# Two MoE products as seven block products each, in place of eight, on one Trainium2 core

## The chip, the core and the metric

The kernel runs on one core of one Trainium2 chip. The metric is device time in microseconds, as the median of some runs. The core has a matrix engine (PE, its weight loads shown apart as PEld), three engines for elementwise work (DVE, ACT, POOL), and SP, which here issues all data transfers. Every engine executes its own instructions in order; waits between engines go through semaphores.

## What is computed

Attention with a sigmoid in place of softmax for 8 batches, 12 heads, 448 positions and head size 64; its result, laid out as 3584 tokens by 768, goes through two matrix products with a gate between them. All is float32.

```
scores = scale * np.matmul(q, k.transpose(0, 1, 3, 2)) - np.log(S)
attn = 1.0 / (1.0 + np.exp(-scores))
attn_out = np.matmul(attn, v)
x = attn_out.transpose(0, 2, 1, 3).reshape(B * S, H * D)
h = x @ w_in                              # 768 -> 2048
g = h * np.clip(h + 3.0, 0.0, 6.0) / 6.0
out = g @ w_out                           # 2048 -> 768
```

The weights arrive as 64-bit floats and are turned into float32 on the chip.

## The kernel before

**Attention** runs in steps: 21 to a batch, 168 in all. A step is four score products (L162) into a PSUM tile `sc` with two buffers, one sigmoid on ACT (L164), and, two steps behind, four products of the result with v (L194). Float32 products run in passes, so the trace has two records for each, 16 records to a step. After each pair of heads, ACT copies one half of the result (L210), DVE adds the other (L211), and DVE splits the sum into a high and a low part of type fp32r (L214, L215).

**The first MoE product** (`moe_in`, L256) works on blocks of 512 tokens (T) and 128 output rows: six chunks of d_model times three products (high by high, high by low, low by high), 18 matmuls of 128x128 weights with 512 moving columns, into one PSUM bank. There are 7 token blocks by 16 row blocks: 2016 matmuls. ACT and DVE make the gate (L260, L261) and SP stores it to DRAM (L263). It is interleaved with attention by batches: three batches, two token blocks, then one batch and one block in turn, and the last block at the end.

**The second product** (`moe_out`, L391) reads the gate back (L347, 1 MB at a time), splits it (L351 on ACT, L352 on DVE), and makes 48 matmuls of 512 columns for each of 42 output tiles: again 2016. DVE scales the result (L398) and SP stores it.

**The weights** are decoded by a chain of one ACT and six DVE or POOL operations, and split (`join_f64`, `split_f32` for w_in, L51 to L67; `split_over` for w_out, L74 to L86). w_in is decoded during the first three batches and the first two blocks; w_out at the end of the first product and the start of the second.

PE, ACT, DVE and POOL follow the order in which the program is written until the last attention batch is done; after that only PE does, and a scheduler sets the others. SP's order is the scheduler's throughout.

## Time and profile before

| | |
|---|---|
| median of 3 runs | 1183.84 us (1183.82 to 1184.26) |
| span of the profiled execution | 1182.4 us, 1.4 us under the median: its own time is not listed apart |
| PE busy | 1172.5 us, 99% |
| DVE, ACT, POOL busy | 427.7, 378.4 and 64.5 us |
| granted PE clock | 1.000 of full |
| moved through DRAM | 129 MB, mean 109 GB/s |

The page gives for each group of instructions its busy time and the mean duration of one in ns. Matmuls are pipelined: the duration of one is longer than the distance to the next, and the distance is what counts. A row of the chain of waits is start, duration and what ran; "xN" counts records.

### The profile page before, as it was taken

The page shows a single profiled execution, that of the slowest core. Times are in us where ns is not written, and L with a number is a line of the kernel's source. Part 1 is how long each engine was busy: PE and PEld are TensorE (multiplying, and loading weights), DVE is VectorE, ACT ScalarE, POOL GpSimd, SP SyncE. Part 2 cuts the span into 40 slices and gives each one's busy share as a digit, 9 for nine tenths or more (in the row PEclk, how much of TensorE's full clock was granted, in tenths as well). Part 3 has the DMA queues.
Part 4 walks back from the last instruction along what each step waited for, and adds up shares of the span by engine and source line. Part 5 has one row for each costly group of instructions (what it writes and reads, how often), then busy time and mean ns, then how long its engine had stood idle before and what let it go on. Part 6 is the DMA issues. An engine that isn't in the chain of part 4 may idle for free.

```text
span 1182.4 us, 16264 instructions
## 1 busy us (share of the span) xinstructions
PE 1172.5 (99%) x6720; PEld 856.1 (72%) x6720; DVE 427.7 (36%) x762; ACT 378.4 (32%) x506; POOL 64.5 (5%) x70
## 2 busy tenths in 40 slices
PE   8999999999999999999999999999999999999998
PEld 3336888748847855874884788888888888888887
DVE  3777772242122123114112699860302203030300
ACT  6885331271163144126116454230201002020200
POOL 1333441000000000000000000000000000000000
PEclk9999999999999999999999999999999999999999
DMA  7655441141132123114112578540321304040000
GB/s 243 197 185 158 161 152 72 63 134 61 71 105 91 63 91 113 63 66 138 63 63 66 176 244 294 167 171 27 109 82 39 154 27 160 27 169 25 21 27 27
DMA packets 52010, 128.99 MB, mean 109 GB/s; under 512 B 9184, under 2 KB 15328, under 8 KB 48352
## 3 DMA queue, kind: packets, MB, share of 16 engines
q1 hardware_dynamic: 51936, 127.95, 31.8%
q8 instruction: 53, 0.87, 0.3%
q14 instruction: 21, 0.17, 0.0%
HBM read 87.56 MB, written 40.37 MB: 108 GB/s over the span
## 4 chain that ended last, share of the span: by engine, by line
PE 99%; ACT 0%; DMA 0%; DVE 0%; issue 0%
PE ph L256 39%; PE po L391 39%; PE sc L162 11%; PE pv L194 11%; ACT a L164 0%; DMA qk<-qk 0%; DVE o L398 0%
## 5 line engine op out<-in xcount | busy, mean ns | idle before, releaser
L256 PE MATMUL ph<-x,wi 128*128 128x512 f32 x2016 | 458.8, 389 | 0.0
L256 PEld LDWEIGHTS ph<-x,wi 128*128 128x128 f32 x2016 | 377.9, 188 | 82.5 <-issue 4.2
L391 PE MATMUL po<-gh,woh 128*128 128x512 f32 x672 | 261.4, 389 | 0.0
L391 PE MATMUL po<-gl,woh 128*128 128x512 f32 x672 | 261.4, 389 | 0.0
L391 PE MATMUL po<-gh,wol 128*128 128x512 f32 x672 | 261.4, 389 | 0.0
L164 ACT ACTIVATE a<-sc,bias_s 128x896 f32<-128x896 f32 x168 | 168.6, 1008 | 53.2 <-PE sc L162 52.0
L261 DVE SCALAR_TENSOR_TENSOR g<-g,ph 128x512 f32<-128x512 f32 x112 | 76.9, 687 | 273.3 <-ACT g L260 273.3
L260 ACT ACTIVATE g<-ph,bias 128x512 f32<-128x512 f32 x112 | 77.2, 689 | 285.1 <-PE ph L256 277.5
L162 PE MATMUL sc<-qk 64*64 64x448 f32 x1344 | 157.5, 545 | 6.2 <-DMA qk<-qk 4.3
L194 PE MATMUL pv<-a,v 64*64 64x448 f32 x1344 | 154.0, 537 | 0.0
L351 ACT CAST gh<-gr 128x2048 fp32r<-128x2048 f32 x28 | 53.6, 1915 | 293.1 <-PE po L391 292.3
L391 PEld LDWEIGHTS po<-gl,woh 128*128 128x128 f32 x672 | 126.1, 188 | 26.2
L391 PEld LDWEIGHTS po<-gh,wol 128*128 128x128 f32 x672 | 126.1, 188 | 26.2
L391 PEld LDWEIGHTS po<-gh,woh 128*128 128x128 f32 x672 | 126.1, 188 | 26.1
L398 DVE TENSOR_SCALAR o<-po 128x512 f32<-128x512 f32 x42 | 29.0, 690 | 294.1 <-PE po L391 294.1
L162 PEld LDWEIGHTS sc<-qk 64*64 64x64 f32 x1344 | 49.5, 134 | 84.3 <-issue 60.3
L194 PEld LDWEIGHTS pv<-a,v 64*64 64x64 f32 x1344 | 50.3, 133 | 76.7 <-issue 71.7
L352 DVE TENSOR_TENSOR gl<-gr,gh 128x2048 fp32r<-128x2048 f32 x28 | 64.1, 2289 | 27.6 <-ACT gh L351 27.6
L211 DVE TENSOR_TENSOR x<-pv,y 128x448 f32<-128x448 f32 (+6 forms) x78 | 32.5, 416 | 113.2 <-ACT y L210 93.0
L61 POOL TENSOR_TENSOR wis<-wis 128x384 f32<-128x384 f32 x32 | 32.4, 1012 | 98.2 <-DVE wis L58 95.8
L215 DVE TENSOR_TENSOR x<-x,x 128x448 fp32r<-128x448 f32 (+6 forms) x78 | 32.8, 420 | 2.7
L67 POOL TENSOR_TENSOR wi<-wis,wi 128x384 fp32r<-128x384 f32 x32 | 32.2, 1019 | 20.2 <-ACT wi L66 17.2
(29 smaller groups left out, 309.0 us busy)
## 6 DMA issues: line engine op xcount, KB each, us to landing
gd<-g SPq DMA_DIRECT2D x112, 256.0 KB, 2.4
gr<-gd SPq DMA_DIRECT2D x28, 1024.0 KB, 5.4
qk<-qk SPq DMA_DIRECT2D x48, 448.0 KB, 3.8
wis<-wi SPq DMA_DIRECT2D x32, 384.0 KB, 3.4
ws<-wo SPq DMA_DIRECT2D x24, 512.0 KB, 4.4
outT<-o SPq DMA_DIRECT2D x42, 256.0 KB, 2.0
v<-vP SPq DMA_DIRECT2D x24, 224.0 KB, 2.6
v<-vP SPq DMA_DIRECT2D x24, 192.0 KB, 3.0
```

The lines of the kernel that those rows point to most:

```text
L61: nc.gpsimd.tensor_tensor(out=a, in0=a, in1=b, op=ALU.add)
L162: nc.tensor.matmul(out, k[halves[r], at_k], q[halves[r]], start=True, stop=True)
L164: nc.scalar.activation(a, sc[:, :, :S], AF.Sigmoid, bias=bias_s, scale=scale)
L194: nc.tensor.matmul(pv[p][r][halves[j], :S], v, a[halves[r], int(r != j) if c is None else j], start=first, stop=last)
L211: nc.vector.tensor_tensor(out=x, in0=p1[:, q0 : q0 + w], in1=y, op=ALU.add)
L215: nc.vector.tensor_tensor(out=xl, in0=x, in1=xh.bitcast(F32), op=ALU.subtract)
L256: nc.tensor.matmul(ph, w[:, cc], x, start=(n == 0), stop=(n == 3 * NCC - 1))
L260: i1 = nc.scalar.activation(g, ph, AF.Relu, bias=bias_3, scale=1.0)
L261: i2 = nc.vector.scalar_tensor_tensor(out=g, in0=g, scalar=6.0, in1=ph, op0=ALU.min, op1=ALU.mult)
L351: nc.scalar.copy(gh, gr)
L352: nc.vector.tensor_tensor(out=gl, in0=gr, in1=gh.bitcast(F32), op=ALU.subtract)
L391: nc.tensor.matmul(po[t, ec], w[:, fc], x[:, u], start=(fc == 0 and n == 0), stop=(fc == NFC - 1 and n == 2))
```

## The change

Both products are made by Winograd's form of Strassen's scheme. A weight matrix is cut into four quarters A11, A12, A21, A22, and the moving matrix into four quarters B11, B12, B21, B22, where the columns are two batches (a *pair*, `p`, 0 to 3; 448 columns each) and the rows the two halves of the contracted dimension. Sums of quarters come first: S1 = A21 + A22, S2 = S1 - A11, S3 = A11 - A21, S4 = A12 - S2, and T1 = B12 - B11, T3 = B22 - B12, T2 = T3 + B11, T4 = B21 - T2. Then there are seven products in place of eight:

M1 = A11 B11, M2 = A12 B21, M3 = S4 B22, M4 = A22 T4, M5 = S1 T1, M6 = S2 T2, M7 = S3 T3.

The results are C11 = M1 + M2, C21 = M1 + M6 + M7 + M4, C22 = M1 + M6 + M7 + M5, C12 = M1 + M6 + M5 + M3. All sums are float32, and each product still consists of three fp32r products.

**Attention** comes first, all 168 steps. x of the first pair stays on the chip; its sums are made by DVE (`x_sums`) and its seven operands split (`x_split`: a cast on ACT, a subtraction on DVE), at steps 45 to 62. x of the other three pairs goes to DRAM and comes back later. In the same time w_in is decoded (16 units of 768 values a partition, one in six steps), its sums are made by POOL, and quarters and sums are stored to DRAM; so are A11 and A12 of w_out.

**The first product** then runs in 112 *slots* (`product`), one for each of 7 products by 16 *quads* (4 row groups by 4 pairs); a slot is 18 matmuls of 448 columns. Accumulators are PSUM tiles A (two buffers), B and D (one each). A holds M1, then M6, M7 and M4 added on top, and ACT copies it in between (`copied`); B holds M2; D holds M5, then M3 on top. DVE adds the copies (`added`), ACT and DVE make the gate (`relu`, `gate`), POOL makes T2 and T3 of the gate (`g_sums`), and SP stores six pieces for each quad. The weights of each slot are loaded five slots ahead and split three slots ahead (`w1_load`, `w1_split`). At the seams between pairs, the seven operands of the next pair are split one by one (in `x_split`), each after the last use of the old one.

**The second product** runs in 56 *units*: seven products (order M1, M2, M6, M7, M5, M4, M3), four pairs, two halves of the contraction; a unit is 36 matmuls of 448 columns. Its moving operand is loaded three units ahead and split two units ahead (`g_load`, `g_split`); for M5 and M4 it is also a difference of two stored pieces. A21 and A22 of w_out are decoded in units 0 to 11, POOL makes the sums in units 6 and 12 (`w2_sums`), SP stores them one unit later, and the weights of each product are loaded back and split at its seam (units 8, 16, ..., 48).

All five engines, SP too, now follow the order written. In the rows below the names are the program's, and the number behind the last underscore is a running count.

**ACT during attention.** Before, some 30 steps in, while w_in is decoded: the sigmoids (L164), copies of the attention result (L210) and the w_in chain (L51, L66).

```order
L164 ACTIVATE a_738<-sc_733,bias_s 128x896
L164 ACTIVATE a_749<-sc_744,bias_s 128x896
L66 CAST wi_595<-wis_596 128x384
L51 ACTIVATE wis_670<-wis_670 128x384
L164 ACTIVATE a_776<-sc_771,bias_s 128x896
L210 COPY y_0_783<-pv_9_714 128x64
L210 COPY y_1_789<-pv_9_714 128x384
L164 ACTIVATE a_800<-sc_795,bias_s 128x896
```

At most two short operations stand between two sigmoids. Now, from step 50 on: sigmoids (L177), copies (L202), decoding (L50) and the casts of the first pair's operands (L69).

```order
L177 ACTIVATE a_948<-sc_943,bias_s 128x896
L69 CAST x_0_952<-xr_0_260 128x1344
L202 COPY y_959<-pv_903 128x448
L177 ACTIVATE a_967<-sc_962,bias_s 128x896
L177 ACTIVATE a_983<-sc_978,bias_s 128x896
L69 CAST x_2_987<-xr_1_735 128x1344
L177 ACTIVATE a_1001<-sc_996,bias_s 128x896
L177 ACTIVATE a_1012<-sc_1007,bias_s 128x896
L69 CAST x_1_1014<-xr_1_416 128x1344
L202 COPY y_1022<-pv_973 128x448
```

A cast of 1344 values stands between every second sigmoid and the next, seven times.

**DVE at a seam between pairs in the first product.** Before, at the end of a batch: the last attention result is added and split, then only gates (L261) follow while the product runs.

```order
L211 TENSOR_TENSOR x_0_4746<-pv_41_4709,y_0_4747 128x384
L214 CAST x_5_4037<-x_0_4746 128x384
L215 TENSOR_TENSOR x_5_4037<-x_0_4746,x_5_4037 128x384
L211 TENSOR_TENSOR x_1_4752<-pv_41_4709,y_1_4753 128x64
L214 CAST x_5_4756<-x_1_4752 128x64
L215 TENSOR_TENSOR x_5_4756<-x_1_4752,x_5_4756 128x64
L261 SCALAR_TENSOR_TENSOR g_0_4778<-g_0_4778,ph_0_4759 128x512
```

No operand is split while the product runs. Now, from the slot of M1 of the last quad of a pair on: operands of the next pair (x_0 is B11, x_1 B21, x_2 B22), gates (L344), weights (w), sums (L362).

```order
L70 TENSOR_TENSOR x_0_4158<-xr_0_0_3572,x_0_4158 128x1344
L344 SCALAR_TENSOR_TENSOR g_6_4130<-g_6_4130,cD_4128 128x896
L70 TENSOR_TENSOR w_4164<-ws_4101,w_4164 128x768
L344 SCALAR_TENSOR_TENSOR g_6_4185<-g_6_4185,A_3937 128x896
L70 TENSOR_TENSOR w_4190<-ws_4132,w_4190 128x768
L362 TENSOR_TENSOR cB_4212<-B_4193,s_7_4156 128x896
L70 TENSOR_TENSOR x_1_4216<-xr_0_1_3574,x_1_4216 128x1344
L344 SCALAR_TENSOR_TENSOR g_7_4214<-g_7_4214,cB_4212 128x896
L70 TENSOR_TENSOR w_4223<-ws_4162,w_4223 128x768
L362 TENSOR_TENSOR cD_4244<-D_4081,u_6_4069 128x896
```

The last row reads the accumulator D that the next M5 overwrites, and all the others stand before it.

**ACT and SP in units 6 and 7 of the second product.** Before, ACT in the second product decodes the rest of w_out and then only casts gates:

```order
L74 ACTIVATE wa_3_6147<-ws_3_6146 128x512
L85 CAST woh_6108<-wa_0_6111 128x512
L85 CAST woh_6108<-wa_1_6123 128x512
L85 CAST woh_6108<-wa_2_6135 128x512
L85 CAST woh_6108<-wa_3_6147 128x512
L351 CAST gh_0_6432<-gr_0_6431 128x2048
```

The decoded parts lie in buffers of their own, and SP loads and stores no weights by way of DRAM. Now, ACT (with what each row waits for):

```order
L69 CAST gx_8_6391<-gr_8_6342 128x1792 [waits DMAHW2_49,DVE_49]
L50 ACTIVATE w2_2_1_6401<-wo_2_1_0_6351 128x512 [waits DMAHW3_49,DMAHW0_49,Pool_49]
L69 CAST gx_9_6450<-gr_9_6394 128x1792 [waits DMAHW4_49,DVE_49,PE_49]
L50 ACTIVATE w2_2_1_6401<-wo_2_1_1_6409 128x512 [waits DMAHW5_49]
L69 CAST w2_1_0_0_6471<-w2s_1_0_6411 128x512 [waits DMAHW6_49]
```

and SP:

```order
L452 DMA w2s_1_0_6411<-dw2_1_0_75 128x1536 [waits DMAHW7_49,DMAHW6_49,DVE_49]
L428 DMA gr_10_6453<-gd_1_1_0_101 128x1792 [waits Activation_49]
L536 DMA dw2_5_0_81<-w2r_0_0_6298 128x1536 [waits DMAHW0_49,Pool_49]
L536 DMA dw2_6_0_83<-w2_2_0_6069 128x1536 [waits DMAHW1_49]
L536 DMA dw2_4_0_79<-w2S1_0_6396 128x1536 [waits DMAHW2_49]
L536 DMA dw2_3_0_77<-w2_3_0_6236 128x1536 [waits DMAHW3_49]
L536 DMA dw2_7_0_85<-w2r_1_0_6300 128x1536 [waits DMAHW4_49,Pool_49]
L248 DMA wo_2_1_2_6467<-wo 128x1024 [waits DMAHW5_49,DVE_49]
```

`w2_2_1` takes the buffer of `w2r_0_0`, in which POOL makes S2 and which SP stores as `dw2_5_0`; behind the ACT row that waits for both stand the cast of unit 9's operand and those of M2's weights (`w2_1_0_0`).

The core of the diff; attention's own lines change little, and the old product functions go.

```diff
-    def moe_in(*blocks):
-        for i, (fc, t) in enumerate(itertools.product(range(NFC), blocks)):
...
-    def moe_out(t, ec, g):
...
+def sums(engine, a11, a12, a21, a22, s1, s2, s3, s4):
+
+    engine.tensor_tensor(out=s1, in0=a21, in1=a22, op=ALU.add)
+    engine.tensor_tensor(out=s3, in0=a11, in1=a21, op=ALU.subtract)
+    engine.tensor_tensor(out=s2, in0=s1, in1=a11, op=ALU.subtract)
+    engine.tensor_tensor(out=s4, in0=a12, in1=s2, op=ALU.subtract)
...
+    for q in range(n - 1):
+        seq += [(M1, q + 1), (M4, q), (M2, q + 1), (M3, q), (M6, q + 1), (M5, q + 1), (M7, q + 1)]
...
+    def ring(name, shape, dtype):
+        return dw.tile(shape, dtype, tag="ring", name=name, bufs=5)
...
+    def x_split(p, k):
+        x = xt[k].tile([P, 2, KC, S], F32R, tag="x", name=f"x_{p}_{k}")
+        split(nc, x[:, 0], x[:, 1], xr[p].pop(k))
+        xts[p, k] = x
...
+    for i, k in enumerate((B11, B22, B21, T3, T1, T2, T4)):
+        on(end0 + 6 + 2 * i, x_split, 0, k)
...
+    def product(i, q, n):
+
+        w, x = wr.pop(n), xts[q // NQ, MOVING[i]]
+        if i == M1:
+            acc["A", q] = bank("sc", 2, f"A_{q}")
+        if i == M2:
+            acc["B", q] = bank("pv0", 1, f"B_{q}")
+        if i == M5:
+            acc["D", q] = bank("pv1", 1, f"D_{q}")
+        t = acc["B" if i == M2 else "D" if i in (M5, M3) else "A", q]
+        for j in range(2):
+            m = 0
+            for kc in range(KC):
+                for wk, xk in ((0, 0), (0, 1), (1, 0)):
+                    nc.tensor.matmul(
+                        t[:, j, :S],
...
+    def copied(q, key):
+        acc[key, q] = temp("a", 4, f"{key}_{q}")
+        nc.scalar.copy(acc[key, q], acc["A", q][:, :, :S])
+
+    def added(q, key, name):
+        c = temp("y", 2, f"c{name}_{q}")
+        nc.vector.tensor_tensor(out=c, in0=acc[name, q][:, :, :S], in1=acc[key, q], op=ALU.add)
+        return c
...
+        for i in range(7):
+            at_slot(last[i, p - 1] + 1, x_split, p, MOVING[i])
...
+        for k, o in enumerate(others):
+            part = t[:, 2 * k : 2 * k + 2]
+            nc.vector.tensor_tensor(out=part, in0=part, in1=o, op=ALU.subtract)
...
+        at_unit(6 * h + 4, w2_reload, h)
+        at_unit(6 * h + 6, w2_sums, h)
+        at_unit(6 * h + 7, w2_store, h)
+    for k, i in enumerate(PHASES[1:]):
+        n = 8 * (k + 1)
+        at_unit(n - 2, w2_load, i, 0)
+        at_unit(n - 1, w2_load, i, 1)
+        at_unit(n - 1, w2_split, i, 0)
+        at_unit(n, w2_split, i, 1)
```

More of the change, by code (lines that the diff above doesn't have):

```diff
@@ new lines, in w2_unit @@
+    def w2_unit(k, h, ec, held):
+        st = staging(f"wo_{k}_{h}_{ec}", [P, FC * P, 2], I32)
+        nc.sync.dma_start(out=st, in_=wo[k, h, :, ec * FC * P : (ec + 1) * FC * P])
+        yield
+        if ec == 0:
+            held[k, h] = ring(f"w2_{k}_{h}", [P, EC, FC * P], F32)
+        yield from decode(nc, st, held[k, h][:, ec])
+        if ec == EC - 1 and k in (A11, A12):
+            nc.sync.dma_start(out=dw2[k, h], in_=held.pop((k, h)))
+    held = {}
+    todo = []
+    for u in range(4 * NQ):
+        todo.append((1 + 6 * u, 4, w1_unit(*divmod(u, 2), held)))
@@ new lines, in g_load @@
+    def g_load(n):
+        if n >= len(units):
+            return
+        i, p, h = units[n]
+        first, second = {T1: (B12, B11), T4: (B21, T2)}.get(MOVING[i], (MOVING[i], None))
+        t = gset[n % 3].tile([P, FC, S], F32, tag="gr", name=f"gr_{n}")
+        nc.sync.dma_start(out=t, in_=gd[p, first, h])
+        others = []
+        if second is not None:
+            for k in range(2):
+                o = ring(f"gr_{n}_{k}", [P, 2, S], F32)
+                nc.sync.dma_start(out=o, in_=gd[p, second, h][:, 2 * k : 2 * k + 2])
+                others.append(o)
+        gr[n] = t, others
@@ new lines, in w2_split @@
+    def w2_split(i, h):
+        st = w2s.pop((i, h))
+        for ec in range(EC):
+            w = xs.tile(
+                [P, 2, FC, P], F32R, tag="xT" if h else "xraw", name=f"w2_{i}_{h}_{ec}", bufs=3 if h else 5
+            )
+            flat = w.rearrange("p t c e -> p t (c e)")
+            split(nc, flat[:, 0], flat[:, 1], st[:, ec])
+            w2[i, h, ec] = w
+    last = {}
+    for n, (i, q) in enumerate(seq):
+        last[i, q // NQ] = n
+    first = {}
+    for n, (i, q) in reversed(list(enumerate(seq))):
+        first[q // NQ] = n
@@ new lines, in tile_kernel, with xt_close @@
+    for p in range(1, NPR):
+        at_slot(first[p - 1] + 2, x_load, p)
+        at_slot(first[p - 1] + 8, x_sum_start, p, first[p - 1] + 9)
+        for i in range(7):
+            at_slot(last[i, p - 1] + 1, x_split, p, MOVING[i])
+    end = len(seq)
+    for h in range(2):
+        at_slot(end - 12 + h, w2_load, M1, h)
+        at_slot(end - 10 + 2 * h, w2_split, M1, h)
+    def xt_close(*ks):
+        for k in ks:
+            xt_ctx[k].close()
+        g_open()
+    for n in range(LA):
+        pass
@@ new lines, in tile_kernel @@
+    for n in range(LA, LA + 2):
+        w1_load(n)
+    p_last = NPR - 1
+    for n, (i, q) in enumerate(seq):
+        for f, a in later.pop(n, []):
+            f(*a)
+        w1_load(n + LA + 2)
+        w1_split(n + LA)
+        product(i, q, n)
+        post(i, q, n)
+        if n == last[M6, p_last]:
+            xt_close(B11, T2)
+            g_load(0)
+        if n == last[M2, p_last]:
+            xt_close(T3, B21)
+            g_load(1)
+        if n == last[M6, p_last] + 2:
+            g_split(0)
+        if n == last[M2, p_last] + 2:
+            g_split(1)
@@ new lines, in tile_kernel @@
+    for n, (i, p, h) in enumerate(units):
+        if n < 2:
+            drain_later()
+        if n == 1:
+            while later:
+                drain_later()
+            tmp_ctx.close()
+            acc_ctx.append(ctx.enter_context(tc.tile_pool(name="acc", bufs=1, side="right", reuse_waits="tile")))
+        g_split(n + 2)
+        g_load(n + 3)
+        for f, a in plan.pop(n, []):
+            f(*a)
+        if h == 0:
+            po[p] = po_pool.tile([P, EC, 512], F32, tag="po", name=f"po_{i}_{p}")
+        x = gs.pop(n)
+        for ec in range(EC):
+            w = w2[i, h, ec]
+            for c in range(FC):
+                for wk, xk in ((0, 0), (0, 1), (1, 0)):
+                    nc.tensor.matmul(
+                        po[p][:, ec, :S],
+                        w[:, wk, c],
+                        x[:, xk, c],
+                        start=h == 0 and c == 0 and xk == 0 and wk == 0,
+                        stop=h == 1 and c == FC - 1 and wk == 1,
+                    )
+        if h == 1:
+            post2(i, p)
```

600 lines of the change are left out of this document (325 added, 275 removed).

## The prediction, as it was put on record

> **What bounds the kernel now.** I read the page's busy times and chain first, then the chain in order of time.
>
> ```profile
> PE 1172.5 (99%) x6720; PEld 856.1 (72%) x6720; DVE 427.7 (36%) x762; ACT 378.4 (32%) x506; POOL 64.5 (5%) x70
> PE 99%; ACT 0%; DMA 0%; DVE 0%; issue 0%
> PE ph L256 39%; PE po L391 39%; PE sc L162 11%; PE pv L194 11%; ACT a L164 0%; DMA qk<-qk 0%; DVE o L398 0%
> ```
> ```profile
> 0.73 3.52 DMA qk<-qk
> 4.30 4.76 PE sc L162 x24
> ...
> 99.41 2.25 PE pv L194 x24
> 101.66 130.82 PE ph L256 x576
> 232.49 0.96 PE sc L162 x8
> ...
> 264.82 65.50 PE ph L256 x288
> ...
> 721.69 456.97 PE po L391 x2016
> ```
>
> PE's matmuls set the end all along. The products take 456.97 / 2016 = 226.7 ns a matmul (130.82 / 576 = 227.1 in the first), 4032 of them 914 us. Attention takes 2.25 / 24 x 16 records = 1.50 us a step.
>
> Why 226.7 ns? Attention's rows tell the rate: four of its 64*64 records run side by side, so 24 in 2.25 us are 375 ns for four; if each streams its 448 columns twice, that is 2.4 columns a ns, and 512 columns would take 213.3. So 13.3 ns come on top. The weight loads could be the cause:
>
> ```profile
> L256 PEld LDWEIGHTS ph<-x,wi 128*128 128x128 f32 x2016 | 377.9, 188 | 82.5 <-issue 4.2
> 740.56 0.39 PE L391 MATMUL po<-gh,woh 128*128 128x512 f32 x1
> 740.57 0.19 PEld L391 LDWEIGHTS po<-gl,woh 128*128 128x128 f32 x1
> 740.79 0.39 PE L391 MATMUL po<-gl,woh 128*128 128x512 f32 x1
> ```
> ```profile
> 101.59 0.30 PEld L256 LDWEIGHTS ph<-x,wi 128*128 128x128 f32 x2 [0.70 <-issue]
> ```
>
> A load starts as its predecessor's matmul starts and lasts 188 ns; the next matmul comes 39 ns after its end. But in the last row two loads of 188 ns end within 0.30 us, so one follows the other by 0.11. A load is then not what 226.7 ns wait for; the columns are.
>
> **Part one: the matmuls.** The order keeps their number (112 x 18 + 56 x 36 = 4032), so it does what it says, and takes the columns from 512 to 448. No row has 448 columns with full-size weights. Lower end: all of 226.7 scales, 198.3 ns. Upper end: nothing does, 226.7. I take the 13.3 ns as fixed, 186.7 + 13.3 = 200.0: a slot is 3.6 us, a unit 7.2, each product 2016 x 0.2 = 403.2 us, together 806.4 against 914.
>
> **Part two: attention.** 168 steps x 1.503 = 252.5 us; the first load 4.3; the cold start costs 4.76 - 2.25 = 2.5. A batch that starts alone, as from 232.49 to 264.82, takes 32.3 us for 21 steps of 1.503 (31.6); five such starts fall away, some 4 us against before. What is new is the load on ACT and DMA.
>
> ```profile
> L164 ACT ACTIVATE a<-sc,bias_s 128x896 f32<-128x896 f32 x168 | 168.6, 1008 | 53.2 <-PE sc L162 52.0
> L74 ACT ACTIVATE wa<-ws 128x512 f32<-128x512 f32 x24 | 16.2, 677 | 43.9 <-DMA ws<-wo 38.9 <-DVE wol L86 3.0 <-DVE wa L77 1.9
> L51 ACT ACTIVATE wis<-wis 128x384 f32<-128x384 f32 x32 | 17.7, 556 | 2.1 <-DVE wis L57 2.1
> L351 ACT CAST gh<-gr 128x2048 fp32r<-128x2048 f32 x28 | 53.6, 1915 | 293.1 <-PE po L391 292.3 <-DMA gr<-gd 0.7
> L85 ACT CAST woh<-wa 128x512 fp32r<-128x512 f32 x24 | 14.8, 616 | 13.4 <-DVE wa L84 13.3
> L210 ACT COPY y<-pv 128x448 f32<-128x448 f32 x12 | 6.3, 526 | 1.2 <-PE pv L194 1.2
> ```
>
> From L351 and L85 a cast costs 0.183 us + 0.846 ns a value: 1.32 us for an operand (1344), 0.83 for a slot's weights (768), 1.70 for a unit's (1792). From L74 and L51, decoding 768 values costs ACT 0.92. In the 14 steps from 50 on (21.0 us) ACT has 14 sigmoids (14.1), seven casts (9.2), 2.3 decodings (2.1) and four copies (2.1): 27.5. Two score buffers give 1.2 us of slack (a step lasts 1.5, a sigmoid 1.0, and the second next step waits for it). So PE waits 6.5 - 1.2 = 5.3 us. Bounds: 0 if idle time around absorbs it, 8 if DVE, as full there (the pair's four sums and seven subtractions, 17 us by the slope below, beside 19 of decoding and adding in 30), adds its own.
>
> ```profile
> 60.00:70.00 10.00, 10.00 (x112) 3.79 (x108) 8.07 (x19) 8.91 (x15) 3.02 (x3) 1.00 0.52 158
> 695.00:705.00 10.00, 10.00 (x46) 8.28 (x45) 9.37 (x19) 5.42 (x8) 0.00 (x0) 1.00 0.94 340
> 705.00:715.00 10.00, 10.00 (x46) 8.29 (x45) 9.97 (x18) 4.41 (x7) 0.00 (x0) 1.00 0.93 317
> ```
>
> These rows by stretches give the busy time of PE, PEld, DVE, ACT and POOL, the granted clock, the DMA engines' busy share and GB/s. From step 42 to 97 the change moves per six steps (9.02 us) 1.18 MB of q, k, v, 0.79 of w_in, 0.79 of stored weights and 0.39 of x: 349 GB/s. The most seen is 340 at 0.94; 83 us stretched by 349/340 become 2 us longer, by 349/317 8. I take 3, nearer the faster row, since transfers here are larger. Attention: 4.3 + 2.5 + 252.5 + 5.3 + 3 = 267.6.
>
> **Part three: the first product.** Work besides PE, by these rows:
>
> ```profile
> L352 DVE TENSOR_TENSOR gl<-gr,gh 128x2048 fp32r<-128x2048 f32 x28 | 64.1, 2289 | 27.6 <-ACT gh L351 27.6
> L86 DVE TENSOR_TENSOR wol<-wa,woh 128x512 fp32r<-128x512 f32 x24 | 16.5, 686 | 0.8 <-ACT woh L85 0.7
> L75 DVE TENSOR_SCALAR wa<-wa 128x512 f32<-128x512 f32 x24 | 10.2, 424 | 7.8 <-ACT wa L74 7.8
> L61 POOL TENSOR_TENSOR wis<-wis 128x384 f32<-128x384 f32 x32 | 32.4, 1012 | 98.2 <-DVE wis L58 95.8 <-issue 2.3
> ```
>
> DVE: 0.151 us + 1.044 ns a value, so 0.95 for weights, 1.09 for 896 values, 1.56 for an operand. A quad lasts seven slots, 25.2 us. DVE then has 7 x 0.95 + 7 x 1.09 = 14.3 us, ACT 7 x 0.83 + 7 x 1.01 = 12.9. In the middle of a pair every result is read within the one slot of slack, and PE runs through. At a seam seven casts (9.2) and subtractions (10.9) come on top within eleven slots. I count slot 0 as that of M1 of the last quad, from 0 us. x_0's cast follows M1's copy (to 5.3) and ends at 6.6; its subtraction, two gates and two weight splits keep DVE until 12.4, though M2 ended at 10.8. Then: sum to 13.5, ReLU on ACT 14.6, cast of x_1 15.9, subtraction 17.6, gate 18.7, weights 19.6, and only then the sum that frees D, at 20.7. M5 was due at 18.0: PE waits 2.8. The same chain with x_3 and x_2 delays the next M5 and M7 by 3.2. Three seams x 6 = 18 us; bounds 0 (the casts fall into ACT's gaps) and 30. First product: 421.2.
>
> **Part four: the second product.** In units 0 to 5 DVE waits 1.7 for the cast, splits (2.0) and decodes 512 values (3.3, three operations at 0.42 and three at 0.69): 7.0 of 7.2, so PE runs through. It waits at seams, where the next weights are split late.
>
> M2 (unit 8): POOL's four sums of 1536 values cost 4 x 4.05 = 16.2 us from the start of unit 6. ACT's decoding in unit 6 writes into the buffer of S2, and so waits for the third sum (12.2) and its store. A store's landing I take as 4 us from loads:
>
> ```profile
> gr<-gd SPq DMA_DIRECT2D x28, 1024.0 KB, 5.4
> ws<-wo SPq DMA_DIRECT2D x24, 512.0 KB, 4.4
> ```
>
> At 16.3 ACT goes on, DVE behind it: decoding 3.3, split of unit 9's operand 2.0, decoding 3.3, first weights 0.7, with 0.7 for ACT ahead: 26.3. Unit 8 was due at 14.4: 11.9 us, and 2.5 for the cold clock. On SP the stores wait for POOL to 16.2, and behind them stand the next load of w_out, M2's second weights and unit 11's operand; with 3.9 MB of stores ahead of them I count them in by 27, when DVE comes to them, so they add nothing. With POOL twice as fast the wait is 6; with DVE held up as well, 20.
>
> M6 (unit 16): the second sums begin at the end of unit 11; from 12.2 on 6.3 MB of stores, output, operands and weights pass at 340 GB/s until 30.7, cast and subtraction 1.3; due at 28.8: 3.2 us.
>
> M5 and M4 (units 32 to 47): a unit's operand costs DVE two differences (2.2), a wait for ACT's cast (1.7) and the split (2.0), 5.9 us; two units 11.8, M5's two results 3.1, so 14.9 plus 4.1 of weights at each seam against 14.4. Carried through in order, unit 33 is 1.9 us late, unit 40 2.3 and unit 41 3.9: 8.1.
>
> Sum: 14.4 + 3.2 + 8.1 = 25.7; second product 428.9, bounds 403 and 455. The end (last sums 3 x 0.62 and an output of 0.7 MB landing in some 3.5) is 5.6.
>
> **The sum.** 267.6 + 421.2 + 428.9 + 5.6 = 1123.3 us of span against 1182.4. The median stands 1.4 above the span, which gives 1124.7: 1125 us, 5% faster.
>
> **The rivals.**
>
> *All of it hidden.* The waits above are walked from durations, and a little slack in each would undo them. For it: before, ACT was 89% busy in the stretch from 60 us and PE did not wait. Against: DVE's order at the seams leaves no way round. 259.3 + 806.4 + 5.6 + 1.4 = 1073 us (1066 at 198.3 ns).
>
> *DVE blocked by POOL.* A DVE copy of 64 values takes longer than one of 192:
>
> ```profile
> L214 DVE CAST x<-x 128x64 fp32r<-128x64 f32 x12 | 5.8, 480 | 0.4
> L214 DVE CAST x<-x 128x192 fp32r<-128x192 f32 x12 | 3.1, 260 | 0.4
> ```
>
> The short ones stand beside POOL's L61 and wait for its end. If that holds for every DVE operation with two inputs too, POOL's sums (2 x 2.4 us a quad, and four of 3.5 a pair) come on top of a DVE that is full at the seams: 5 to 8 us each, about 20 in all: 1145. The Trainium skill ("SBUF — State Buffer", "Who interferes with whom") says just that: a VectorE instruction with two SBUF inputs and a GpSimd one that reads SBUF hold a shared port in turn, and the second blocks fully. The trace agrees for copies; no row here has a two-input operation starting inside a POOL one, so this rival keeps a chance of its own.
>
> *The weight load sets the pace* (the other side). If a matmul needs its load's 188 ns plus 39 of hand-over, 448 columns also take 226.7 ns. For it: the load starts with the matmul before, and 39 ns are left unexplained. Against: the loads 0.11 us apart. Then the matmuls stay at 914; longer slots take the lateness at most seams, leaving 9 and 15: 267.6 + 914 + 24 + 5.6 + 1.4 = 1213, slower. It decides from (1183.8 - 1.4 - 5.6 - 267.6 - 43.7) / 4032 = 215 ns on.
>
> **How the numbers follow.** Forecast 0.55 (1095 to 1155), hidden 0.13, blocked 0.15 (1135 to 1170), weight load 0.11, and 0.06 for waits more than twice as long as walked, around 1170 to 1195. The likeliest gives 1125. A range of 1070 to 1175 leaves out the weight load, most of the 0.06 and a little below, 0.17 in all. 0.2% is about what a measurement tells from no change: faster 0.55 + 0.13 + 0.15 + 0.02 = 0.85, same 0.02, slower 0.13.
>
> **What would show it.** The distance of matmuls in the groups of A and po: 200 ns, or 227. The chain of waits should name DVE and ACT at three seams of the first product, and ACT, POOL and a store before unit 8; 252 to 268 us of attention with waits on L177 near steps 50 to 64. PE idle should be some 55 us in all. The forecast is wrong if slots without a seam last over 3.7 us, or if attention waits for DMA from step 42 on.

## The result, and the profile after

The changed kernel takes 1162.67 us (median; 1161.45 to 1164.15) against 1184.05 for the kernel before on the same chip: a ratio of 0.9824, 95% interval 0.981 to 0.9837. It is 1.8% faster; the forecast was 5%. The profiled execution has a span of 1159.8 us where the sum gave 1123.3, so 36.5 us went somewhere that the sum does not have.

First the page of the changed kernel: busy times, and the chain that ended last, by engine and by line.

```profile
PE 1101.3 (95%) x6720; PEld 864.8 (75%) x6720; DVE 734.7 (63%) x710; ACT 557.5 (48%) x612; POOL 205.8 (18%) x90
PE 32%; DVE 5%; DMA 3%; issue 3%; ACT 2%; POOL 2%; POOLq 0%; SPq 0%; DVEq 0%; ACTq 0%
```

Before, PE was 99% of the chain over the whole span. Here the chain could be followed back only to 584 us, so its shares cover half of the span: PE's 32% are two thirds of what was followed, and DVE, DMA, ACT and POOL have most of the rest. It says nothing of attention, which is read from the lists of waits instead. What PE waited for, by its list of waits (total us, times, longest; the longest totals):

```profile
PE sc L175 <- ACT a L177: 12.4, 11, 3.8
PE po L634 <- DVE w L70: 10.7, 5, 5.8
PE D L333 <- DVE cD L362: 10.2, 8, 2.4
PE po L634 <- ACT w L69: 7.9, 3, 4.6
PE sc L175 <- DMA qk<-qk: 5.5, 3, 4.4
```

L175 is attention, L333 the first product, L634 the second. The span comes apart at the first matmul of each stage; inside a product I take as pace the mean distance of matmul starts below 215 ns, and as waits what larger distances have above 200.

| term of the sum | forecast, us | measured, us | difference |
|---|---|---|---|
| first load | 4.3 | 4.4 | +0.1 |
| attention, first score to first product | 263.3 | 279.9 | +16.6 |
| first product, 2016 matmuls | 403.2 (200.0 ns) | 411.7 (204.2 ns) | +8.5 |
| its waits | 18 | 16.8 | -1.2 |
| between the products | 0 | 2.8 | +2.8 |
| second product, 2016 matmuls | 403.2 (200.0 ns) | 413.9 (205.3 ns) | +10.7 |
| its waits | 25.7 | 24.6 | -1.1 |
| end | 5.6 | 6.0 | +0.4 |

So two terms make 35.8 of the 36.5 us: attention, and the pace of a matmul. The waits inside the products came out as walked in total, and the piece of the chain before unit 8 nearly so (rows of "issue" under 0.1 us are left out):

```profile
760.07 3.53 POOL w2S L528
763.67 5.18 POOL w L529
768.93 3.54 POOL w2r L530
772.53 3.49 POOL w2r L531
776.05 0.67 ACT w L50
...
785.57 0.70 DVE w L70
786.31 16.03 PE po L634 x70
```

From the start of POOL's sums to PE's unit 8 the prediction had 26.3 us; the rows have 26.2. But it let ACT wait for the third sum and the landing of its store, and the chain goes through the fourth sum, which reads the same buffer. By the trace the store landed at 775.75 and the fourth sum ended at 776.02: the wait that ended last was another one, of nearly the same length.

**Attention.** SyncE's list of waits up to 284 us shows where the time begins:

```profile
SPq L242 <- DVE wA L63: 68.0, 8, 11.9
SPq L205 <- DVE xr L203: 43.2, 8, 10.8
SPq L243 <- POOL wS L78: 36.2, 8, 7.7
SPq L154 <- PE sc L175: 23.0, 20, 4.8
SPq L254 <- DVE w L63: 19.3, 3, 7.3
```

L242 and L243 store decoded weights, L205 the attention output, L254 decoded weights of w_out. All of them stand in SP's order ahead of loads (L154, L231), and before them SP waits 167 us for DVE and POOL (the rows without L154). ACT in turn waits for the loads of w_in that come late, and the sigmoids stand behind its decodings:

```profile
ACT wA L50 <- DMA wi<-wi: 13.8, 7, 4.2
```

The list of SP's own work round 80 us (start, duration, instruction) shows one such place, and PE's list what follows from it:

```profile
70.60 0.60 SPq L154 DMA_DIRECT2D qk<-qk  x1
83.18 0.38 SPq L242 DMA_DIRECT2D dw<-wA  x1
91.34 0.38 SPq L243 DMA_DIRECT2D dw<-wS  x1
91.81 1.87 SPq L154 DMA_DIRECT2D qk<-qk  x1
94.22 0.42 SPq L231 DMA_DIRECT2D wi<-wi  x1
```
```profile
97.13 0.98 PE L175 MATMUL sc<-qk 64*64 64x448 f32 x8 [0.87 <-DMA qk<-qk]
```

No load is issued between 71 and 91.8 us, and at 97 PE waits for q and k. The pairs of stores L242 and L243 come every twelve steps, and so does the lateness: by the starts of their scores, steps 21, 33, 45, 57, 69, 81, 93 and 105 together last 11.6 us longer than 1.503 us each.

### The profile page after: what moved, and what is told of

The parts are those of the page before. It is cut to its first block, busy times and chain, and to the rows that moved or that the text cites. A ratio compares the mean times of both kernels' runs of the same rounds, so it can differ in the third digit from the quotient of the medians.

```text
span 1159.8 us, 16568 instructions
## 1 busy us (share of the span) xinstructions
PE 1101.3 (95%) x6720; PEld 864.8 (75%) x6720; DVE 734.7 (63%) x710; ACT 557.5 (48%) x612; POOL 205.8 (18%) x90
## 5 line engine op out<-in xcount | busy, mean ns | idle before, releaser
L634 PE MATMUL po<-gx,w 128*128 128x448 f32 x2016 | 419.9, 370 | 21.2 <-DVE w L70 10.7
L634 PEld LDWEIGHTS po<-gx,w 128*128 128x128 f32 x2016 | 380.3, 189 | 60.8 <-DVE w L70 12.8
L333 PE MATMUL A<-x,w 128*128 128x448 f32 x1152 | 241.2, 367 | 0.7 <-ACT s L358 0.7
L333 PEld LDWEIGHTS A<-x,w 128*128 128x128 f32 x1152 | 216.0, 188 | 21.3 <-ACT s L358 1.1
L69 ACT CAST gx<-gr 128x1792 fp32r<-128x1792 f32 x56 | 94.8, 1694 | 258.8 <-PE po L634 98.8
L70 DVE TENSOR_TENSOR gx<-gr,gx 128x1792 fp32r<-128x1792 f32 x56 | 122.2, 2183 | 121.7 <-ACT gx L69 121.6
L177 ACT ACTIVATE a<-sc,bias_s 128x896 f32<-128x896 f32 x168 | 168.1, 1010 | 46.6 <-PE sc L175 44.2
L70 DVE TENSOR_TENSOR w<-ws,w 128x768 fp32r<-128x768 f32 x112 | 148.4, 1334 | 53.4 <-ACT w L69 53.4
L175 PE MATMUL sc<-qk 64*64 64x448 f32 x1344 | 163.7, 549 | 18.0 <-ACT a L177 12.4
L333 PE MATMUL D<-x,w 128*128 128x448 f32 x576 | 126.4, 374 | 10.2 <-DVE cD L362 10.2
L333 PEld LDWEIGHTS D<-x,w 128*128 128x128 f32 x576 | 110.1, 192 | 22.7 <-issue 13.0
L175 PEld LDWEIGHTS sc<-qk 64*64 64x64 f32 x1344 | 51.9, 135 | 99.4 <-issue 56.3
L69 ACT CAST w<-ws 128x768 fp32r<-128x768 f32 x112 | 92.1, 828 | 19.9 <-DMA ws<-dw 19.8
L333 PE MATMUL B<-x,w 128*128 128x448 f32 x288 | 61.4, 366 | 0.0
L333 PEld LDWEIGHTS B<-x,w 128*128 128x128 f32 x288 | 54.1, 188 | 4.7
L344 DVE SCALAR_TENSOR_TENSOR g<-g,cD 128x896 f32<-128x896 f32 x32 | 46.4, 1451 | 16.2 <-ACT g L353 16.2
```

Source lines behind the costliest of these rows:

```text
L69: nc.scalar.copy(hi, a)
L70: nc.vector.tensor_tensor(out=lo, in0=a, in1=hi.bitcast(F32), op=ALU.subtract)
L175: nc.tensor.matmul(out, k[halves[r], at_k], q[halves[r]], start=True, stop=True)
L177: nc.scalar.activation(a, sc[:, :, :S], AF.Sigmoid, bias=bias_s, scale=scale)
L333: nc.tensor.matmul(t[:, j, :S], w[:, wk, j, kc], x[:, xk, kc], start=i in (M1, M2, M5) and m == 0, stop=m == 3 * KC - 1, skip_group_check= ...
L344: nc.vector.scalar_tensor_tensor(out=r, in0=r, scalar=6.0, in1=h, op0=ALU.min, op1=ALU.mult)
```

## The experiments

Each ratio is to the kernel before on the same chip (1183.1 to 1183.9 us). Times are medians of four executions where an interval is given, else of one; stages, waits and units are read from the one execution that was profiled. Lines of kernels with later stores lie some ten further on: L343 is the first product there, L644 the second (L645 in the last kernel), L372 the sum into `cD`.

### What a matmul costs at 448 columns

Streams of matmuls with nothing else of the task; a stream's weights and operands are made once.

```diff
+    for name, n, m, busy in STREAMS:
...
+                    for wk, xk in ((0, 0), (0, 1), (1, 0)):
+                        nc.tensor.matmul(po[:m, :n], w[:, wk, c : c + m], x[:, xk, kc * n : (kc + 1) * n], ...)
```

> This kernel leaves the task out: it only runs 14 streams of 180 float32r matmuls each, weights and operands made once, in the order of the changed kernel (high x high, high x low, low x high), each stream with its own number of columns (512, 480, 448, 416, 384, 320, 256) and, in three, with 64 or 32 of the 128 weight columns. Between two streams PE waits a microsecond or two for a copy on ACT. In two streams (448 and 512) DVE, POOL and the DMA engines are kept busy. Theory (a hand-over between load and matmul that no other engine has a part in): 512 at 226.7 ns and 448 at 202 to 207 ns with nothing else running, the same beside busy engines, and the part over the columns (13.3 ns at 512) larger at 448 and larger still at 384, since the weight load comes nearer to the column time. With 64 or 32 weight columns 448 falls to 200 ns or below if the load is what is left over. Rival 1 (other engines or DMA disturb PE): 448 alone at 200.0 ns, 202 to 207 only in the busy stream. Rival 2 (a fixed price per matmul): 13.3 ns over the columns at every width, 200.0 at 448, 173.3 at 384. Rival 3 (the load alone sets a floor of some 200 ns): 384, 320 and 256 all stay at 200 or more.

Measured, as mean distance of the last 120 starts of a stream (464, 456, 432, 400, 352, 304, 288, 192 and 128 are from the next kernel):

| columns | 512 | 480 | 464 | 456 | 448 | 432 | 416 | 400 | 384 | 352 | 320 | 304 | 288 | 256 | 192, 128 |
|---|---|---|---|---|---|---|---|---|---|---|---|---|---|---|---|
| ns | 226.7 | 217.0 | 211.1 | 207.4 | 202.7 or 206.7 | 195.5 | 188.9 | 181.5 | 173.3 | 159.3 | 146.7 | 140.0 | 132.6 | 120.0 | 111.7 |
| over columns / 2.4 | 13.3 | 17.0 | 17.8 | 17.4 | 16.0 or 20.0 | 15.5 | 15.6 | 14.9 | 13.3 | 12.6 | 13.3 | 13.3 | 12.6 | 13.3 | 31.7, 58.3 |

The profile's stretches show the same in counts (PE's busy time and records first; a record lasts some 0.37 us, so a stretch counts that much more):

```profile
170.00:195.00 25.00, 25.00 (x146) 25.00 (x145) 0.00 (x0) 0.00 (x0) 0.00 (x0) 1.00 0.00 1
370.00:400.00 30.00, 30.00 (x150) 27.81 (x149) 0.00 (x0) 0.00 (x0) 0.00 (x0) 1.00 0.00 1
408.00:438.00 30.00, 30.00 (x147) 27.25 (x146) 29.66 (x11) 0.00 (x0) 29.22 (x11) 1.00 0.00 1
445.00:475.00 30.00, 30.00 (x134) 24.82 (x134) 29.59 (x11) 0.00 (x0) 29.22 (x11) 1.00 0.00 1
```

The first row is 384 columns (25.36 / 146 = 173.7), the second 448 with PE alone (30.37 / 150 = 202.5), the third 448 beside DVE and POOL at full load (206.6), the fourth 512 beside them (226.6). The transfers meant for the last two ran early instead, beside the first stream of 448, which took 202.7 as well. The fixed price of rival 2, on which my 200.0 rested, is exact at 512, 384, 320, 304 and 256, is 0.7 ns too much at 352 and 288, and fails at 448, 480 and all widths tried between 400 and 480. Rival 3 falls: 256 columns take 120.0. Fewer weight columns (64 or 32), whose loads take 134 or 108 ns instead of 188, leave 448 at 202.2, so the theory's remark on the load falls too. Whether the busy engines made 206.7 of 202.7 was left to the next kernel.

```diff
+    ("a", 448, ""), ("b", 448, "pad"), ("c", 448, "one_x"), ("d", 448, "one_w"), ("e", 448, "banks"),
...
+    ("l", 288, ""), ("m", 192, ""), ("n", 128, ""), ("o", 448, "wait1"), ("p", 448, "wait2"), ("q", 448, "wait3"),
```

> This kernel leaves the task out again: streams of 180 float32r matmuls, PE alone. Seven streams have 448 columns: as in the changed kernel, with operand rows 512 apart instead of 448, with always the same moving operand, with always the same weights, with two banks of PSUM in turn, and three entered after waits of different length; one more is interrupted by short waits. The other widths are 464, 456, 432, 400, 352, 304, 288, 192 and 128. Theory (the pace is a cycle into which PE and its loads fall after a wait, whatever the data): all streams of 448 at one of two paces, 202.7 or 206.7, whichever the wait before them leads to, and the interrupted one can change from one to the other at a wait; 192 and 128 at the columns plus 13.3 ns (93.3, 66.7) until a load of 188 ns no longer fits behind them. Rival 1 (addresses of the operands): rows 512 apart, or always the same operand, give 200.0. Rival 2 (writing PSUM): two banks in turn give 200.0. Rival 3 (weights change): the same weights give 200.0.

PE was alone here, and both paces came: 206.67 with always the same weights and after the shortest added wait, 202.67 as in the changed kernel, with rows 512 apart, one moving operand, two banks, and after the two longer waits. Stretches of the streams after a wait for two copies and after one for a single copy (25.37 us / 125 = 203.0 ns and / 123 = 206.3):

```profile
515.00:540.00 25.00, 25.00 (x125) 23.16 (x124) 0.00 (x0) 0.00 (x0) 0.00 (x0) 1.00 0.00 1
475.00:500.00 25.00, 25.00 (x123) 22.71 (x122) 0.00 (x0) 0.00 (x0) 0.00 (x0) 1.00 0.00 1
```

None ran at the 200.0 of the three rivals. The interrupted stream ran at 202.7, after a short wait at 206.7, after the next at 202.7 again. So at 448 columns PE falls after a wait into one of two cycles and stays in it; in the changed kernel it changes between them at waits alone, and after the last wait at a seam it held 206.67 to the end of the first product. Which wait leads to which cycle was not found. The theory's sentence on 192 and 128 columns was off: they stop at 111.7, not at 93.3 and 66.7.

The second product had 205.33 everywhere, which is neither. Three kernels looked for the reason.

```diff
+        nj, nk = (3, 4) if kind in ("second", "w_as_first") else (2, 3)
...
+                        if kind == "second":
+                            wt = v[:, wk, kc * P : (kc + 1) * P]
+                        else:
+                            wt = w[:, wk, (kc if nk == 4 else j * KC + kc) * P :][:, :P]
```

> This kernel leaves the task out: streams of 180 matmuls with 448 columns, as in the first product (groups of 9 to a bank, weights' low parts 896 values behind the high ones) and as in the second (groups of 12, three banks, low parts 512 behind), entered after waits of one to three copies, some beside busy ACT, DVE and DMA. In the task the second product always ran at 205.33 ns, whatever the wait. Theory (the layout of weights and moving operands takes part in the cycle): 205.33 in the streams laid out as in the second product, 202.67 or 206.67 in the others. Rival 1 (groups of 12 or three banks): 205.33 wherever these stand. Rival 2 (work of the other engines): 205.33 in the busy streams alone.

All eleven streams ran at 202.67, in either layout, in groups of 9 or 12, on three banks and beside busy engines. The streams were to be entered after waits, but results in two buffers let PE run on, so of entries it shows little. Layout, groups and busy engines are out as causes.

```diff
-        g_split(n + 2)
-        g_load(n + 3)
-        for f, a in plan.pop(n, []):
-            f(*a)
...
-        x = gs.pop(n)
+        x = gs[n % 3]
...
-            w = w2[i, h, ec]
+            w = w2[M1, h, ec]
```

> The kernel in which POOL does no sums (1134.1 us, second product 438.5), with the second product left alone with PE: all 56 units take the operands of the first three units and M1's weights, and decoding, sums, stores, loads and splits behind them are left out, so that the output is that of other operands. Only the results' additions and the output's transfers remain. If other engines or transfers set the 205.33 ns of that product: 202.67 or 206.67 here. If the place of its operands in memory does: 205.33 still. The 25 us of waits fall to 2 or less either way.

Measured: 415.2 us for the second product, waits 1.5, the pace still 205.33. Other engines are not the reason. So the operands were put elsewhere:

```diff
+                rw.append(ring(f"rw_{ec}", [P, 2, FC, P], F32R))
+                nc.scalar.copy(rw[ec], w2[M1, 0, ec].bitcast(F32))
+            rx = ring("rx", [P, 2, S], F32R)
...
+            w = rw[ec] if part in (1, 2) else w2[M1, h, ec]
```

> The kernel whose second product is left alone with PE, which still ran at 205.33 ns, with the operands of its units in other places: units 0 to 13 as there, 14 to 27 with weights copied into the buffers that the first product's weights had, 28 to 41 with those weights and one moving operand copied there too, 42 to 55 with that moving operand and the second product's own weights. Values are those of other operands, as before. If the weights' place sets the cycle: 202.67 or 206.67 in the second and third stretch. If the moving operand's place does: in the third and fourth. If neither: 205.33 in all four, and the cause is in the stream of instructions and stays open.

One stretch of each quarter, from this kernel's view by stretches:

```profile
700.00:790.00 90.00, 90.00 (x440) 82.38 (x439) 3.12 (x2) 5.17 (x4) 0.00 (x0) 1.00 0.04 16
800.00:890.00 90.00, 90.00 (x446) 83.54 (x445) 9.35 (x6) 0.00 (x0) 0.00 (x0) 1.00 0.02 8
910.00:990.00 80.00, 80.00 (x396) 74.25 (x396) 13.82 (x10) 0.00 (x0) 0.00 (x0) 1.00 0.10 35
1000.00:1090.00 90.00, 90.00 (x440) 82.38 (x439) 9.73 (x12) 0.00 (x0) 0.00 (x0) 1.00 0.13 49
```

90.37 / 440 = 205.4 and 90.37 / 446 = 202.6: by the starts, 205.33, 202.67, 202.67, 205.33. The weights' buffers decide, and the moving operand's make no difference. The weights of the second product lie in the buffers that held x (5376 bytes a partition each), those of the first in buffers of 6144. Which property of the place it is was not tried.

### Attention: what SyncE waits for

```diff
             sums(nc.gpsimd, *(a[:, k] for k in range(4)), *(s[:, k] for k in range(4)))
-            yield
+            for _ in range(5):
+                yield
...
             if k == KC - 1 and b >= 2:
-                nc.sync.dma_start(out=xd[b, u], in_=xr.pop((b, u)))
+                on(n + LAG + 4, x_store, b, u)
```

> The changed kernel, but in attention the stores of decoded weights and of the attention output are issued four steps later in SP's written order, nothing else moved. Theory (SP stands still before stores whose sums and additions POOL and DVE have not finished, and the loads behind them come late): the 280 us from the first score to the first product fall by 8 to 12 us, about 1152 us in all. Rival 1 (ACT and DVE are overfull with the first pair's operands): within 3 us of 1162.7. Rival 2 (DMA bandwidth): within 3 us, and the stretch from 80 to 100 us stays as it was.

Measured: 1149.19 us (its four runs spread from 1143.1 to 1153.9), ratio to before 0.9703 (0.966 to 0.9746). In the profiled execution, the fastest of the four, attention takes 264.0 us instead of 279.9, against 263.3 forecast; by the medians the whole gains 13.5. Both are more than the 8 to 12 expected. Nothing but four steps in the place of the stores was changed, so their waits in SP's order cost 15.9 us. SP still waits over 100 us before these stores, but the loads are out by then: its own waits for a free buffer of q and k (L154) rise from 23.0 to 75.8 us. The eight steps that were 11.6 us too long are 0.1 us too long. PE's list up to the first product:

```profile
PE pv L195 <- DVE xr L206: 4.8, 4, 1.9
PE sc L175 <- DMA qk<-qk: 4.2, 1, 4.2
PE sc L175 <- ACT a L177: 0.6, 2, 0.4
```

The 12.4 us "<- ACT" of the changed kernel are down to 0.6 although ACT has the same work, and ACT waits for no load of w_in any more: its sigmoids had been late because decodings ahead of them in its order waited for late loads. The one load that PE waits for is the first.

```diff
-        on(end0 + 6 + 2 * i, x_split, 0, k)
+        on(end0 + 6 + 4 * i, x_split, 0, k)
```

> The changed kernel, but the seven casts and subtractions of the first pair's operands are four steps apart instead of two (steps 50 to 74). Theory (SP stands still): 2 to 4 us less, since DVE finishes sums and additions a little earlier and SP waits less. Rival 1 (ACT and DVE overfull; I had counted 5.3 us for it): 5 to 10 us less, 1153 to 1158. Rival 2 (DMA bandwidth): no difference.

> Both edits, later stores and operands four steps apart. Theory (SP) and rival 1 together: 12 to 16 us less, about 1148, attention near 265 us. If bandwidth is the limit: no more than 3 us less, and the DMA engines near 0.95 busy where PE waits.

Spread alone: 1163.37 us, ratio 0.9818 (0.9802 to 0.9834), attention 279.9 as before. Both: 1143.47, ratio 0.9657 (0.9639 to 0.9674), attention 260.0. Spread alone changed nothing, which only the bandwidth rival had named; the overload that I had put at 5.3 us shows once SP no longer holds PE up, at 4.0 us (264.0 to 260.0, one profiled execution each; the next seven kernels with spread operands, from the seams' section to the last one, have 259.1 to 260.6). Two waits at one place do not add. Of the 260.0, some 5 us stand over the 255.0 of steps and cold start, and no run takes them apart. Bandwidth is not what held the changed kernel up: a different order alone made it faster, and with both edits the stretch from 160 to 180 us moves more than the changed kernel's did:

```profile
160.00:180.00 20.00, 18.31 (x196) 7.24 (x188) 6.34 (x9) 12.44 (x15) 3.92 (x4) 1.00 0.75 275
```
```profile
160.00:180.00 20.00, 20.00 (x219) 8.12 (x215) 11.91 (x22) 16.52 (x21) 0.00 (x0) 1.00 1.00 363
```

The first row is the changed kernel, the second the one with both edits; the last two numbers are the DMA engines' share and GB/s. 363 is above the 340 that I had taken as the most to be had, and PE is busy throughout.

### The seams of the first product: POOL's lock

From here every kernel starts from the one with both edits (1143.5 us; first product 432.6, waits in it 18.1).

```diff
-        nc.gpsimd.tensor_tensor(out=t3, in0=quad[q, B22], in1=quad[q, B12], op=ALU.subtract)
+        nc.vector.tensor_tensor(out=t3, in0=quad[q, B22], in1=quad[q, B12], op=ALU.subtract)
...
-        gen = x_sums(nc.gpsimd, p)
+        gen = x_sums(nc.vector, p)
```

> The kernel with later stores and the first pair's operands four steps apart (1143.5 us, first product 432.6), with one more edit: the two sums per quad and the four sums per later pair run on DVE instead of POOL. Theory (POOL's sums hold the port that DVE's operations with two inputs need: a weight subtraction takes 1.35 us there instead of 0.95): DVE's operations get shorter, the 11.4 us of waits for D's sum at the seams fall to 4 or less, first product 421 to 426, 1133 to 1138 in all. Rival (no such lock; DVE at the seams is simply full): DVE has 2.2 us more a quad and 6.2 a pair, the seams get 2 to 6 us longer.

The other way round, more work for POOL:

```diff
-            split(nc, x[:, 0], x[:, 1], xr[p].pop(k))
+            split(nc, x[:, 0], x[:, 1], xr[p].pop(k), nc.gpsimd if p else nc.vector)
```

> The same kernel as a start (1143.5), with the seven subtractions of the later pairs' operands on POOL instead of DVE. Theory (POOL locks DVE out): POOL holds the port for 3.5 us where DVE needed 1.6 to 1.8, so the waits at the seams (18 us over the pace) stay or grow. Rival (DVE is simply full at the seams, as I walked it): 11 us of DVE's work go at each seam, and the waits fall under 6 us.

Groups of DVE's weight subtraction, first as a start, then with the sums on DVE, then with the operands' subtractions on POOL; the numbers behind the bar are busy us, mean ns of one, and idle us ahead:

```profile
L70 DVE TENSOR_TENSOR w<-ws,w 128x768 fp32r<-128x768 f32 x112 | 150.4, 1352 | 53.6 <-ACT w L69 53.6
```
```profile
L70 DVE TENSOR_TENSOR w<-ws,w 128x768 fp32r<-128x768 f32 x112 | 106.0, 953 | 48.7 <-ACT w L69 48.7
```
```profile
L70 DVE TENSOR_TENSOR w<-ws,w 128x768 fp32r<-128x768 f32 x112 | 192.7, 1731 | 64.9 <-ACT w L69 64.9
```

And PE's waits for D's sum by its list of waits, as a start, with the sums on DVE and with the subtractions on POOL:

```profile
PE D L343 <- DVE cD L372: 11.4, 8, 2.4
```
```profile
PE D L343 <- DVE cD L372: 8.0, 7, 1.4
```
```profile
PE D L343 <- DVE cD L372: 18.9, 9, 3.6
```

More work on DVE made its weight subtraction shorter (953 ns, the 0.95 us of the forecast), and work taken from DVE made it longer (1731). The kernel that both start from shows why within one trace: from 266 to 690 us, 65 of these subtractions run clear of POOL's and take 953 ns, and 44 overlap one of POOL's and take 1.97 us in the mean. A gate with both inputs in SBUF (`g<-g,cD`) takes 1.09 us clear of POOL and 3.98 beside it, but the sum `cD<-D,u`, which has one input in PSUM, 1.09 either way. So it is not a general slowdown. With the sums on DVE the first product's waits fall from 18.1 to 11.4, that for D's sum from 11.4 to 8.0, and the whole to 1137.79 us, ratio 0.9602 (0.9586 to 0.9618). Of the 9.8 us that the product became shorter, 6.7 are waits and 3.1 the pace (204.3 to 202.7), which is the cycle that PE happened to fall into. The second product, not edited, is 4.1 us longer in this execution; 2.9 of them are in unit 0, where the clock was granted at half for 6.8 us after the wait of 3 us between the products; in the kernel that this one starts from, the same wait was followed by the full clock. I had expected waits for D of 4 or less. With subtractions on POOL one execution took 1157.47, the product 442.2 with 29.9 of waits, where the rival (DVE is full) had under 6. The Trainium skill ("SBUF — State Buffer", "Who interferes with whom") says that a VectorE instruction with two SBUF inputs and a GpSimd one that reads SBUF exclude each other; these two runs agree, at 0.40 us a weight subtraction (1352 to 953).

### The waits of the second product

```diff
     def w2_sums(h):
...
-        t = nc.gpsimd
+        t = nc.vector
```

> The same kernel as a start (1143.5, second product 438.5), with the sums of w_out's blocks on DVE instead of POOL. Theory (unit 8 waits, through ACT's decoding, for POOL's third sum and its store): four sums of 1536 values take 7 us on DVE and not 17, the 11.2 us before and after unit 8 fall to about 3, and with the clock not dropping the second product takes 425 to 430, 1131 to 1136 in all. Rival (DVE, which decodes and splits in units 6 and 7, gets 7 us later by the sums): unit 8 is as late as before, within 3 us of 1143.5.

Measured: 1136.08 us, ratio 0.9596 (0.9577 to 0.9615), and a span 5.1 us shorter, of which the second product gave 2.8 (435.7) and the first, which was not edited, 2.8 through its pace and waits. Lateness round unit 8 fell only from 12.7 to 11.5 us (units 7 and 8 over 36 x 205.33 ns): four sums of 1.77 us, two decodings and M2's weights now stand in a row on DVE. The theory had the wrong successor; the rival named the right one. That the total lies in the theory's range is in part luck: the second product missed its 425 to 430, and half of the gain is in a product that was not edited.

```diff
-            at_unit(max(0, 6 * h + e - 1), next, gen, None)
-            at_unit(6 * h + e, drain, gen)
+            at_unit(max(0, 8 * h + e - 1), next, gen, None)
+            at_unit(8 * h + e, drain, gen)
```

> All edits so far together (later stores, first operands four steps apart, the sums of both products on DVE), and the decoding and sums of the second half of w_out two units later, so that they do not stand ahead of M2's weights. Theory (units 7 and 8 wait because DVE does sums and two decodings before it splits M2's weights): the 13 us lost around unit 8 fall to 2 or less, M6's seam (unit 16) takes 3 to 8, second product 425 to 432, first product 423, attention 260, all in all 1118 to 1126. Rival (M6 gives it all back, as its sums come two units later): 1130 or more, with unit 16 or 17 late by 10.

> The same, but with the sums of w_out's blocks on POOL, as in the changed kernel. If the order of decoding is what mattered: unit 8 is on time here too. If POOL's speed matters: the sums of the second half take 17 us from the start of unit 14, M6's second weights are due at unit 17, 21.7 us later, with a store and a load of 4 us each between them, and unit 17 is 5 to 10 us late.

```diff
-            sums(nc.gpsimd, *(a[:, k] for k in range(4)), *(s[:, k] for k in range(4)))
+            sums(nc.vector, *(a[:, k] for k in range(4)), *(s[:, k] for k in range(4)))
```

> The same as the first of this call, and w_in's sums in attention on DVE too, so that POOL does no sums. If POOL's lock on DVE still costs attention something: attention falls from 260 to 257 or 258. If DVE is the fuller of the two in attention: 260 to 264. All in all within 4 us of the first.

The first diff is that of the first two kernels, which differ in the engine of w_out's sums, the second that of the third. The first, without POOL in either product: 1136.16 us, ratio 0.9596 (0.958 to 0.9612). Units 8 and 9 are 4.0 and 3.7 late, 16 and 17 6.4 and 2.4: the second product takes 441.6. Round unit 8, 7.7 us are lost where the theory had 2 or less, and the rest of the gain went to M6, as the rival had it. With POOL's sums: 1137.53 in one execution, units 8 and 9 6.4 and 3.5 late, unit 16 8.8, so neither the order of decoding alone nor POOL's speed alone sets these seams. With no sums on POOL at all, w_in's included: 1134.11 (0.9562 to 0.9632 of before), attention 259.7, second product 438.5. The chain of this last kernel names what has taken DVE's and POOL's place:

```profile
748.43 10.30 DMA gr<-gd
759.60 23.99 PE po L644 x106
...
809.25 6.16 DMA dw<-w2r
815.43 10.92 DMA w2s<-dw
827.04 98.70 PE po L644 x468
```

The loads of operands and weights last 10 us and more (the median is 6.0 for operands, 7.5 for weights), behind five stores of 0.79 MB that are issued at once.

```diff
-        at_unit(8 * h + 7, w2_store, h)
+        for e, k in enumerate((S2, S3, S1, A22, S4)):
+            at_unit(8 * h + 7 + (e if h == 0 else 2 * e), w2_store, h, k)
```

> The kernel in which POOL does no sums (1134.1 us), with the five stores of each half's sums in the second product put one or two units apart instead of all at once, the one that M6 needs first in the second half. Theory (with POOL gone from the path, M2's and M6's weights and operands arrive late because 3.9 MB of stores stand in front of them): the 8 us around unit 8 and the 9 at units 16 and 17 both halve, second product 428 to 432, 1124 to 1128 in all. Rival (DVE's chain of sums, decoding and splits sets both seams): within 3 us of 1134.

Measured: 1121.35 us, ratio 0.9481 (0.9465 to 0.9497), the fastest of all. Unit 9 is 1.5 us late and unit 16 1.2; the second product takes 423.1, below what was expected. The rival is out. PE's list of waits is now led by DVE at the seams, M5's and M4's differences, and attention's first load:

```profile
PE D L343 <- DVE cD L372: 6.9, 7, 1.4
PE po L645 <- DVE w L70: 5.8, 5, 1.5
PE sc L175 <- DMA qk<-qk: 4.5, 1, 4.5
```

Against the changed kernel its span is 41.4 us shorter: 20.4 in attention, 6.0 in the first product, 15.1 in the second. All of it comes from the order of the work and from the engine that does the sums.

## Why the prediction was wrong, step by step

- **The direction and the count of matmuls** were right: PE is still busy 95% of the span, and 4032 matmuls of 448 columns replaced as many of 512. Both signs that were named of the forecast being wrong came: slots without a seam last 3.72 us in the cycle of 206.67 ns, and PE waits 0.87 us for q and k at 97 us, past step 42.
- **The pace was mis-sized.** "I take the 13.3 ns as fixed, 186.7 + 13.3 = 200.0": measured 204.2 and 205.3, 19 us in all. The streams show that 13.3 holds at 512, 384, 320 and 256 and not at 448, where PE runs in a cycle of 202.67, 206.67 or, with the weights in x's old buffers, 205.33 ns. Why these cycles exist stays open. One width in the trace of before could not show that; the bounds (198.3 to 226.7) held it.
- **Attention failed as a step.** "What is new is the load on ACT and DMA", with 5.3 us for the casts and 3 for bandwidth. Neither was the cause of the excess: 15.9 of the 16.6 us were SP standing before stores whose sums were late, with the loads behind them. The sum has no term for it. I had named what is queued behind a waiting store for unit 8, and not for the eight pairs of stores in attention. The 5.3 us of overload measured 4.0 once SP was free, and the DMA engines moved 363 GB/s, so 340 was no limit; whether the 3 us for bandwidth were paid, no run shows.
- **The seams** came out in total (16.8 us for 18), but not for the reason given alone: my walk used DVE's undisturbed durations, and these are longer beside POOL. Without POOL, and with more work on DVE, 9.9 to 11.4 us remain. The walk was too long by about as much as the lock, which it left to a rival, added (6.7 us), so the total was luck. That rival's mechanism was real; its price (20 us on top) was not, and that 1162.7 lies in its 1135 to 1170 is chance, since attention and the pace made the difference.
- **Units 8 and 16** were right in place, and in size only together. M2's seam lost 12.7 us for 14.4, M6's 5.3 for 3.2, M5's and M4's 6.3 for 8.1: the 24.6 us of waits in the second product come near 25.7 because the misses cancel. The chain before unit 8 has 26.2 us for 26.3, with the fourth sum in place of the store's landing. What hid behind them was not seen: with POOL off the path DVE's row of sums and decodings took its place, then the stores. "They add nothing" held only as long as POOL was later.
- **The weight load as pace** and **all of it hidden** are out: 256 columns take 120.0 ns, and PE waits in every stage.

## What to carry to other kernels

Where a queue is written in order, a store that waits for a slow sum holds back every load behind it; four steps of delay for the store gave 15.9 us of attention here. Before giving sums to an engine because it is idle, ask what they do to its neighbour: here DVE was better off making POOL's sums itself than working beside them, by 6.7 us of waits in the first product. Count an operation's duration beside its neighbour, not alone. Before cutting the width of a matmul, time a bare stream of that width, with its weights where they will lie.

## What the hardware showed that I had not expected

At 448 columns PE has several stable paces, 202.67, 205.33 and 206.67 ns. It changed between the first and the last at waits alone and kept them for hundreds of matmuls, and 205.33 went with the buffers of its weights; 512, 384, 320 and 256 showed one each, columns / 2.4 plus 13.3 ns. A narrower weight tile (64 or 32 columns) hardly shortens a matmul of 448 (202.2 for 202.7), and 64 columns lengthened one of 512 (230.0 for 226.7). Matmuls of 128 and of 192 columns take the same 111.7. After some of the waits of about 2 us and more, not after all, the granted clock is 0.5 for 3.4 us or a multiple of it; a matmul then takes 373.3 ns, which is exactly 448 columns at 1.2 a ns, with nothing on top.
